# First chunk's q/k products tile by tile, with its statistics interleaved and the q/k weights in four column blocks

## The chip, the cores and the metric

The kernel runs on one core of one Trainium2 chip. The metric is the device time of one execution in microseconds (us), as a median over the executions of a kernel. The profile's span, from the first to the last instruction, is about 1.8 us shorter than that time. Ratios and intervals use fast executions alone.

## The reference

A sequence of 2048 rows of 512 numbers is normalised; a windowed attention runs beside a two-stage network with its own normalisation, and the two are multiplied. Cut to what matters here:

```python
x = A_x                                   # 1 x 2048 x 512, bf16
xn = _layernorm(x)                        # (x - mean) / sqrt(var + 1e-5)
qkv = (xn @ wqkv)                         # 512 x 1536: q, k, v; 32 heads of 16
logits = q . k over 8 keys, 2 apart, masked where the key lies before row 0
s = softmax(logits) @ v @ wo
h = gelu(_layernorm(xn) @ w1)             # a second layernorm of the same rows
...                                       # shifts, w2, third layernorm, w3, w4
return x + s * silu(...)
```

## The kernel before

Rows are worked on in four chunks (c = 0 to 3) of four tiles (j = 0 to 3) of 128 rows. The scheduling is manual: the order of the calls is the order of the instructions on each engine. For each tile, VectorE takes statistics, GpSimd raises to the power -0.5, VectorE normalises, TensorE transposes, ScalarE copies; then come the products with the q/k weights. The second layernorm needs no second pass: its factor follows from the first one's variance (`ln_again`), and is multiplied in by one large VectorE product for each chunk (`stage_m`), which the w1 products read.

```python
for c in range(NCH):                            # loads, all on the SP queue, in this order
    ...                                         # x of chunk c
    if c == 0:
        nc.sync.dma_start(out=wqk_sb[:, :, 0:D], in_=wqkv_v[:, :, 0:D])
        nc.sync.dma_start(out=wqk_sb[:, :, D : 2 * D], in_=wqkv_v[:, :, D : 2 * D])
    if c == 1:
        nc.sync.dma_start(out=w1_sb, ...)
...
def mask_coefs():                               # GpSimd, four small operations
def mask_poly(w):                               # GpSimd, three operations on 128x64
    gp.tensor_scalar(out=g, in0=c, scalar1=f2, scalar2=f1, op0=ALU.mult, op1=ALU.add)
    gp.tensor_tensor(out=g, in0=g, in1=c, op=ALU.mult)
    gp.tensor_scalar(out=g, in0=g, scalar1=f0, scalar2=None, op0=ALU.add)
def rsqrt_eps(dst, var):                        # chunks 1 to 3: L280 and L281
    nc.gpsimd.tensor_scalar(out=dst, in0=var, scalar1=EPS, scalar2=None, op0=ALU.add)
    nc.gpsimd.tensor_tensor(out=dst, in0=dst, in1=nhalf[...], op=ALU.pow)
def ln_first(j):                                # chunk 0, tile by tile
    nc.vector.bn_stats(...); nc.vector.bn_aggr(...)
    nc.vector.tensor_scalar(out=r, in0=mv[:, j, 1:2], scalar1=EPS, ...)
    nc.gpsimd.tensor_tensor(out=r, in0=r, in1=nhalf[:, 0:1], op=ALU.pow)
def stage_m(c):                                 # VectorE, the product of two SBUF inputs
    nc.vector.tensor_tensor(out=xn2T[c], in0=xnT[p][:, :, cs], in1=rrep..., op=ALU.mult)
...
    ln_first(0)
    ln_first(1)
    mask_coefs()
    first_n(0)                                  # norm 0
    first_t(0)                                  # transposes and copy
    warm(1)
    ...
    ln_first(2)
    mask_poly(0)
    parts = [qk_pair(0, a, 2) for a in range(3)]  # products in halves of 256 rows
    parts[0][0]()
    ...
    ln_again(0)
    mask_poly(1)
    ln_stats(1, 0, 2)
    ln_stats(1, 2, 4)
    ln_again(1)
    v_ones()                                    # two memsets on GpSimd
    ...
    stage_m(0)
    ln_norm(1)
    ...
    ln_stats(2, 0, 2); stage_w1(0, 0); ...; ln_stats(2, 2, 4); ln_norm(2)
    ...
    row_turn(2); turn(); row_fill(2)
    stage_m(1)
    ...
    stage_w1(1, 0)
```

The softmax here doesn't subtract the row's maximum and nothing guards it: scores larger than these inputs give would overflow.

## Time and profile before

| what | value |
|---|---|
| time, median of 3 | 203.36 us (203.36 to 203.42) |
| span of the profile | 201.7 us |
| TensorE busy | 194.3 us (96%) |
| VectorE, ScalarE, GpSimd busy | 133.8, 131.4, 73.3 us |
| TensorE dense from | 10.47 us on |
| w1 of chunk 1 starts | 27.51 us |

A line of the timeline reads: start, duration, engine, source line, operation, output and inputs with their shapes, how many instructions were joined, and in brackets the idle time just before with what ended it. A line of the chain reads: start, duration, what. PE is TensorE, DVE is VectorE, POOL is GpSimd.

### The profile page before, as it was taken

The numbers are of one execution on the slowest core, as the hardware profiler recorded it, in microseconds if no ns is written. First come the engines' busy times: TensorE is split into PE (matmuls) and PEld (weight loads), VectorE is DVE, ScalarE is ACT, GpSimd is POOL, SyncE is SP. The second block draws the span as 40 slices with busy tenths as digits, with TensorE's granted clock in tenths as the row PEclk, the third lists the DMA queues.
The fourth block names the chain that finished last, engine by engine and source line by source line (L and its number), as shares of the span: only waits on it lengthen the run. The fifth ranks groups of instructions, "written<-read, shape, count | busy, mean of one in ns | idle before, by whom it ended". The sixth has DMA issues, their size and how long they took to land.

```text
span 201.7 us, 4915 instructions
## 1 busy us (share of the span) xinstructions
PE 194.3 (96%) x1967; PEld 94.8 (47%) x1967; DVE 133.8 (66%) x263; ACT 131.4 (65%) x155; POOL 73.3 (36%) x146
## 2 busy tenths in 40 slices
PE   7699999999999999999999999999999999999991
PEld 2475445444444444444444444444445444444461
DVE  5788889734298988885560501288577968676683
ACT  2367665859988888896655566998788879222120
POOL 4789516300023095887364000001930590800000
PEclk9999999999999999999999999999999999999999
DMA  5993257367750086698657955789330141555221
GB/s 139 359 349 96 64 147 135 62 103 113 136 229 5 17 196 86 98 215 184 184 119 210 243 163 118 108 199 348 79 54 5 40 98 31 115 166 165 81 78 54
DMA packets 33734, 27.17 MB, mean 135 GB/s; under 512 B 14720, under 2 KB 31624, under 8 KB 33712
## 3 DMA queue, kind: packets, MB, share of 16 engines
q1 hardware_dynamic: 31520, 23.64, 46.0%
q0 software_dynamic: 2048, 3.09, 8.4%
q8 instruction: 15, 0.25, 0.6%
q10 hardware_dynamic: 144, 0.13, 0.2%
q14 instruction: 7, 0.06, 0.1%
HBM read 12.82 MB, written 4.98 MB: 88 GB/s over the span
## 4 chain that ended last, share of the span: by engine, by line
PE 91%; DVE 3%; POOL 2%; DMA 1%; issue 1%; ACT 0%; DVEq 0%
PE w_ps L567 19%; PE w_ps L530 17%; PE qk_ps L432 9%; PE v_ps L596 8%; PE w_ps L488 7%; PE w_ps L465 7%; PE s_ps L621 7%; PE wo_ps L742 7%; PE o_ps L644 5%; PE qk_ps L450 4%; PE w_ps L547 1%; DMA arena<-in_A_x_dram 1%; DVE l0s L311 1%; POOL l0r L315 1%; PE tr_ps L384 1%; DVE arena L747 1%
## 5 line engine op out<-in xcount | busy, mean ns | idle before, releaser
L626 ACT ACTIVATE arena<-s_ps 128x960 bf16<-128x960 f32 (+1 forms) x68 | 62.7, 975 | 12.3 <-PE s_ps L621 12.3
L567 PE MATMUL w_ps<-arena 128*128 128x512 bf16 (+1 forms) x173 | 40.1, 368 | 0.0
L534 ACT ACTIVATE arena<-w_ps 128x1024 bf16<-128x1024 f32 x20 | 20.5, 1025 | 13.3 <-PE w_ps L530 13.3
L686 POOL DMA_DIRECT2D arena<-orw x48 | 24.9, 526 | 5.3 <-DVE orw L656 5.3
L567 PEld LDWEIGHTS <-arena 128*128 128x128 bf16 x187 | 17.6, 98 | 18.9
L530 PEld LDWEIGHTS <-arena 128*128 128x128 bf16 x160 | 15.5, 98 | 19.2 <-issue 0.8
L752 POOL TENSOR_TENSOR arena<-arena 128x512 bf16<-128x512 bf16 x6 | 7.2, 1225 | 43.3 <-DVE arena L586 32.3
L432 PE MATMUL qk_ps<-arena 128*128 128x512 bf16 (+1 forms) x112 | 20.4, 333 | 0.5 <-ACT arena L328 0.5
L656 DVE CAST orw<-o_ps 128x960 bf16<-128x960 f32 (+1 forms) x17 | 19.7, 1157 | 1.5 <-PE o_ps L644 1.4
L601 DVE CAST v_aug<-v_ps 128x512 bf16<-128x512 f32 x17 | 11.7, 691 | 11.0 <-PE v_ps L596 11.0
L582 ACT ACTIVATE arena<-arena 128x512 bf16<-128x512 bf16 (+1 forms) x9 | 5.2, 583 | 20.4 <-DVE arena L573 20.4
L573 DVE TENSOR_TENSOR arena<-w_ps,arena 128x512 bf16<-128x512 f32 (+1 forms) x17 | 11.2, 659 | 10.3 <-PE w_ps L567 10.3
L530 PE MATMUL w_ps<-arena 128*128 128x512 bf16 x80 | 17.8, 379 | 0.1
L596 PE MATMUL v_ps<-wv_sb,arena 128*128 128x512 bf16 x68 | 17.5, 380 | 0.0
L530 PE MATMUL w_ps<-arena,arena 128*128 128x512 bf16 x80 | 17.4, 379 | 0.0
L621 PEld LDWEIGHTS <-arena 32*128 32x128 bf16 x544 | 10.2, 92 | 14.5 <-issue 14.4
L280 POOL TENSOR_SCALAR l3r<-l3m 128x1 f32<-128x1 f32 (+2 forms) x11 | 2.7, 244 | 38.6 <-DVE l3m L289 38.5
L621 PE MATMUL s_ps<-arena 32*128 32x120 bf16 (+1 forms) x544 | 15.9, 213 | 0.0
L488 PE MATMUL w_ps<-arena 128*128 128x512 bf16 x64 | 15.3, 380 | 0.0
L492 DVE TENSOR_TENSOR arena<-w_ps,arena 128x512 bf16<-128x512 f32 x16 | 10.4, 684 | 7.2 <-PE w_ps L488 7.2
L439 ACT CAST arena<-qk_ps 128x1024 bf16<-128x1024 f32 x11 | 11.1, 1019 | 6.0 <-PE qk_ps L432 6.0
L465 PE MATMUL w_ps<-arena 128*128 128x512 bf16 x64 | 14.8, 379 | 0.0
(108 smaller groups left out, 270.4 us busy)
## 6 DMA issues: line engine op xcount, KB each, us to landing
x1n_dram<-arena SPq DMA_DIRECT2D x5, 512.0 KB, 3.4
arena<-in_A_x_dram SPq DMA_DIRECT2D x4, 512.0 KB, 8.0
arena<-in_A_x_dram SPq DMA_DIRECT2D x6, 256.0 KB, 6.8
out_dram<-arena SPq DMA_DIRECT2D x6, 256.0 KB, 2.1
arena<-in_B_w_dram SPq DMA_DIRECT2D x1, 1376.0 KB, 6.7
arena<-in_B_w_dram SPq DMA_DIRECT2D x1, 1280.0 KB
arena<-arena SPq DMA_DIRECT2D x16, 72.0 KB, 2.5
arena<-arena SPq DMA_DIRECT2D x16, 68.0 KB, 3.0
```

Of the source, the lines that this page charges most:

```text
L432: nc.tensor.matmul(pt[:, b, hh * w : (hh + 1) * w], lhsT=wqk_sb[:, dt, nt * P : (nt + 1) * P], rhs=xnT[p][:, dt, k * CH + hh * w : k * CH ...
L465: nc.tensor.matmul(pt[:, b, :], lhsT=w1_sb[:, dt, g * P : (g + 1) * P], rhs=xn2T[c][:, dt, :], start=(dt == 0), stop=(dt == ND - 1),)
L488: nc.tensor.matmul(pt, lhsT=w2_src(p, g, m0), rhs=w2_sb[:, g, :], start=(g == 0), stop=(g == ND - 1))
L530: nc.tensor.matmul(pt[:, ft % 2, :], lhsT=w3_sb[:, dt, ft * P : (ft + 1) * P], rhs=x1nT[c][:, dt, :], start=(dt == 0), stop=(dt == ND - 1),)
L534: nc.scalar.activation(h3(c, 2 * a, 2), pt, AF.Gelu_apprx_tanh)
L567: nc.tensor.matmul(pt, lhsT=h3(c, ft, 1)[:, 0, jj * P : (jj + 1) * P], rhs=w, start=(ft == 0), stop=(ft == NF - 1),)
L596: nc.tensor.matmul(vp[:nk, :], lhsT=xnT[p][:, dt, k0 : k0 + nk], rhs=wv_sb[:, dt, :], start=(dt == 0), stop=(dt == ND - 1),)
L621: nc.tensor.matmul(st[:nk, b, i * nq : (i + 1) * nq], lhsT=kT[e][r : r + 32, dt, k0 : k0 + nk], rhs=qT[e][r : r + 32, dt, q0 : q0 + nq], s ...
L626: nc.scalar.activation(prv[:nk, 2 * h : 2 * h + 2], st[:nk, :, 0 : 4 * nq], AF.Exp, scale=SCALE)
L656: nc.vector.tensor_copy(out=orw[p, r][:, :, :, q0 - ra : q0 - ra + nq], in_=op[:, :, 0 : 4 * nq].rearrange("p j (s q) -> p j s q", q=nq),)
L686: nc.gpsimd.dma_start(out=oT[p][DH * hh : DH * (hh + 1), :, ra : ra + rw], in_=orw[p, r][32 * cg : 32 * cg + DH, jj],)
L742: nc.tensor.matmul(pt, lhsT=oT[p][:, dt, i * P : (i + 1) * P], rhs=wo_sb[:, dt, ds], start=(dt == 0), stop=(dt == ND - 1),)
```

## The change

The intent is to make TensorE dense earlier. Each tile's q/k products follow its transposes at once, as pieces of 128 columns; the statistics of the next tile are put between the steps of the tile before; the weights come in four column blocks so that the first products need not wait for a half. To clear the way for chunk 0's powers, the mask's coefficients and polynomials move behind chunk 1's statistics, and the two memsets go later still.

```diff
-            nc.sync.dma_start(out=wqk_sb[:, :, 0:D], in_=wqkv_v[:, :, 0:D])
-            nc.sync.dma_start(out=wqk_sb[:, :, D : 2 * D], in_=wqkv_v[:, :, D : 2 * D])
+            for n in range(0, 2 * D, 2 * P):
+                nc.sync.dma_start(out=wqk_sb[:, :, n : n + 2 * P], in_=wqkv_v[:, :, n : n + 2 * P])
 ...                       (first_s and first_a: ln_first in two parts;
 ...                        qk_first: a pair of products for columns lo to hi)
     ln_first(0)
-    ln_first(1)
-    mask_coefs()
+    first_s(1)
     first_n(0)
     first_t(0)
+    first_a(1)
+    first_s(2)
     warm(1)
     first_n(1)
     first_t(1)
-    warm(1)
-    ln_first(2)
-    mask_poly(0)
-    parts = [qk_pair(0, a, 2) for a in range(3)]
-    parts[0][0]()
-    ln_first(3)
+    first_a(2)
+    qa = [qk_first(a) for a in range(3)]
+    for a in range(3):
+        qa[a](0, P)
+    first_s(3)
     first_n(2)
     first_t(2)
-    parts[1][0]()
+    for a in range(3):
+        qa[a](P, 2 * P)
+    first_a(3)
 ...                       (tile 3 likewise)
     ln_again(0)
+    ln_stats(1, 0, 2)
+    mask_coefs()
+    qa[0](3 * P, CH)
+    stage_r(0)
+    for a in (1, 2):
+        qa[a](3 * P, CH)
+    ln_stats(1, 2, 4)
+    stage_m(0)
+    ln_again(1)
+    mask_poly(0)
     mask_poly(1)
-    ln_stats(1, 0, 2)
-    ln_stats(1, 2, 4)
-    ln_again(1)
-    v_ones()
 ...
     ln_again(2)
+    v_ones()
     stage_w1(0, 1)
```

More of the change, by code (lines that the diff above doesn't have):

```diff
@@ L309, in ln_first, with first_s, first_a @@
             lns[0] = [(0, TPC, first["mv"], first["r"])]
+        first_s(j)
+        first_a(j)
+    def first_s(j):
+        nc.vector.bn_stats(out=first["st"][:, j, :], in_=xn[0][:, j, :])
+    def first_a(j):
         st, mv, rstd = first["st"], first["mv"], first["r"]
-        nc.vector.bn_stats(out=st[:, j, :], in_=xn[0][:, j, :])
         nc.vector.bn_aggr(out=mv[:, j, :], in_=st[:, j, :])
@@ L443, in qk_pair, with qk_first, part @@
         return [lambda hh=hh: part(hh) for hh in range(halves)]
+    def qk_first(a):
+        pt = psa("qk_ps")
+        def part(lo, hi):
+            for b in range(2):
+                nt = 2 * a + b
+                for dt in range(ND):
+                    nc.tensor.matmul(
+                        pt[:, b, lo:hi], lhsT=wqk_sb[:, dt, nt * P : (nt + 1) * P],
+                        rhs=xnT[0][:, dt, lo:hi], start=(dt == 0), stop=(dt == ND - 1),
+                    )
+            if hi == CH:
+                dst, n0 = qk_dst(0, 2 * a)
+                nc.scalar.copy(out=dst[:, n0 : n0 + 2, 0:CH], in_=pt)
+        return part
     def qk_one(c, nt):
@@ L784 @@
     first_t(3)
-    parts[2][0]()
+    for a in range(3):
+        qa[a](2 * P, 3 * P)
     ln_again(0)
-    mask_poly(1)
-    ln_stats(1, 0, 2)
-    ln_stats(1, 2, 4)
-    ln_again(1)
-    v_ones()
-    parts[0][1]()
-    stage_r(0)
-    stage_m(0)
+    ln_stats(1, 0, 2)
[8 more added lines that the diff above has]
+    mask_poly(0)
+    mask_poly(1)
     ln_norm(1)
-    parts[1][1]()
-    parts[2][1]()
     qk_pair(0, 3)[0]()
```

## The prediction

> **What bounds the kernel now.** I read the page first (busy shares and the 40 slices), then the chain in order of time, then the timeline of the first 35 us by engine.
>
> ```profile
> PE 194.3 (96%) x1967; PEld 94.8 (47%) x1967; DVE 133.8 (66%) x263; ACT 131.4 (65%) x155; POOL 73.3 (36%) x146
> ...
> PE   7699999999999999999999999999999999999991
> ```
>
> TensorE is nearly never idle, except in the first two slices of 5.04 us, which is where the change works. The chain shows where the idle time stops:
>
> ```profile
> 9.42 0.55 POOL l0r L315
> 9.97 0.03 issue
> 10.00 0.42 DVE arena L319
> 10.42 0.04 issue
> 10.47 0.40 PE tr_ps L327 x4
> 10.87 1.75 PE qk_ps L432 x16
> 12.61 0.22 PE rrep_ps L406 x4
> 12.84 3.47 PE qk_ps L432 x24
> 16.31 1.73 PE w_ps L465 x8
> 18.04 0.89 PE tr_ps L384 x16
> 18.93 1.73 PE w_ps L465 x8
> 20.66 6.91 PE qk_ps L432 x32
> 27.56 3.56 PE w_ps L465 x16
> ```
>
> Until 10.47 us the end hangs on VectorE and GpSimd (statistics, power, norm of each of four tiles). From then on TensorE runs without a gap. So the most the change can give is how much earlier that dense stretch begins, as long as it then stays dense. The timeline shows a second limit almost hidden behind it:
>
> ```profile
> 22.20 0.73 POOL L281 TENSOR_TENSOR l1r<-l1r,nhalf 128x2 f32<-128x2 f32 x1
> 22.97 0.74 DVE L335 TENSOR_SCALAR arena<-arena,l1m,l1r 128x512 bf16<-128x512 bf16 x2 [0.28 <-POOL l1r L281]
> ...
> 25.95 0.31 DVE L345 STREAM_TRANSPOSE r2t<-r2w 128x128 bf16<-128x128 bf16 x1 [0.92 <-POOL r2w L374]
> 26.18 1.18 DVE L416 TENSOR_TENSOR arena<-arena 128x2048 bf16<-128x2048 bf16 x1
> ...
> 27.51 3.61 PE L465 MATMUL w_ps<-arena 128*128 128x512 bf16 x16
> ```
>
> The product L416 of chunk 1 ends at 26.18 + 1.18 = 27.36, and the w1 matmuls that read it start at 27.51. TensorE had only about 0.15 us to spare there. VectorE got there through chunk 2's norm, which waited for GpSimd's power at 22.97. If this side does not come earlier, TensorE cannot either.
>
> **What the Trainium skill says.** "TensorE: Matmul & The Clock Gate", section "Wait — 56ns, not 53.3ns?", gives warm start-to-start times of 55.6 ns at 128 columns and 215.7 ns at 512. The trace agrees: 16 transposes in 0.89 us are 55.6 ns each, 8 matmuls of 512 in 1.73 us are 216 ns each. "DMA: Bandwidth & Descriptors", section "Specifications", puts the smallest transfer for line rate at 512 B; the new weight blocks have rows of exactly 512 B instead of 1 KB, and no transfer of this trace has that size. "SBUF — State Buffer", section "SBUF: two separate sides", says that VectorE operations with two SBUF inputs and GpSimd operations exclude each other. The trace agrees:
>
> ```profile
> 14.31 1.18 POOL L280 TENSOR_SCALAR l1r<-l1m 128x2 f32<-128x2 f32 x1
> ...
> 34.57 2.30 POOL L374 TENSOR_TENSOR r2b<-r,nhalf 128x4 bf16<-128x4 f32 x1 [1.59 <-DVE r L368]
> ```
>
> The first takes 0.22 us elsewhere and the second 1.05; both began just after an L416 product (14.18 and 34.40) and lasted until it was done and their own time had passed.
>
> **The change part by part.**
>
> *The tiles' statistics.* After, VectorE does statistics 0, statistics 1, norm 0, aggregate 1, statistics 2, norm 1, and so on. Row durations: statistics 0.68, aggregate 0.18, small add 0.15, power on GpSimd 0.58, norm 0.41. From small add to power is 0.24, from power's end to norm 0.03, from a norm's start to the next VectorE start 0.32. Norm 0 no longer waits behind tile 1's aggregate: its power ends at 4.82, so it starts at 4.85 (5.07 before). Aggregate 1 follows at 5.17, add 5.38, power 5.62 to 6.20, norm 1 at 6.24 (5.94 before, so 0.3 later). Norm 2 then comes at 7.62 (8.28) and norm 3, behind the four small mask operations, at 9.03 (10.00). Tile 3 gains about 1.0 us.
>
> *The products.* The same 48 products of 256 columns become 96 of 128: at 55.6 against 108.5 ns (24 matmuls before: 16 x 0.1085 + 8 x 0.216 = 3.46) this adds 96 x 0.0556 - 48 x 0.1085 = 0.13 us of TensorE, and one warm-up matmul of 0.22 goes. In order: transposes 1 at norm 1 + 0.47 = 6.70; 24 products of tile 0 from 6.93 to 8.27; transposes 2 (ready 8.09) to 8.49; tile 1 to 9.83; transposes 3 (ready 9.58) to 10.05; tile 2 to 11.39; the first eight of tile 3 to 11.83; the row product to 12.06; 16 more to 12.95; the fourth pair 8 x 0.216 to 14.68. TensorE reaches w1 of chunk 0 at 14.7 instead of 16.31.
>
> *Whether w1 can start.* It needs the product L416, behind ScalarE's eviction (0.91 to the next start) and copy of the row (0.59): 11.87 + 0.91 + 0.59 + 0.05 = 13.4, ends 14.63. Just in time. So TensorE alone is 1.6 us ahead at this point.
>
> *The weights.* The loads drain in order. Summing the windows of 0.5 us gives 1.59 MB by 7.5 us, when both old halves are through; the second was landed about 0.65 later. The third new block (columns 512 to 767) completes the first 1.31 MB, read by some 6.65 and landed at 7.3, an estimate from these windows. It is needed at about 7.8. Rows of 512 B could eat that half microsecond, but no more than the slack that TensorE has later.
>
> *GpSimd.* This is where the change pays. Between the four powers GpSimd now idles, where it used to do the mask's coefficients (0.98) and first polynomial (1.41). These and the second polynomial (1.34) move behind chunk 1's statistics; the two memsets L273 (0.99) go later. Chunk 0's powers end at 8.97, its second rsqrt takes 2.02 to 10.99. Chunk 1's first pair waits for VectorE: 11.14 to 12.19; coefficients to 13.17; the second pair's L280 to 13.40. Its power (L281) would start at 13.49, as L416 starts at 13.4, and would be held until 14.63: end 15.36. Then chunk 1's second rsqrt, 2.55 as before, to 17.9; both polynomials to 20.65, or 21.2 as their last step meets the two-input mask add L241 at 20.07. Only then come chunk 2's statistics: first pair done 22.2, second 23.3.
>
> *Back on the path.* Before, that second pair was done at 22.93 and chunk 1's w1 began 27.51; now 23.3 makes w1 begin at 27.9. TensorE gets there at 20.66 - 1.6 + 6.91 = about 26.0 and waits nearly 2 us. Sum of this path: +0.4 us. If the power at 13.49 slips in just before L416, only 0.4 us instead of 1.2 is lost on GpSimd, the polynomials end near 20.0, chunk 2's second power near 22.6 and w1 begins at 27.2: -0.3 us. Everything after w1 follows TensorE and only shifts.
>
> **The rivals.**
>
> *The gain goes through.* VectorE, if GpSimd were never late, would reach chunk 1's L416 some 0.9 to 1.0 us earlier (its own work is unchanged; chunk 0's L416 comes 0.8 earlier and a wait of 0.28 goes). For it: the author moved the memsets out of GpSimd's way, and before, GpSimd only held norm 2 back by 0.28. Against it: 2.75 us of polynomials now sit exactly in front of the power that norm 2 waits for, and only 0.99 was taken out. It would give 202.4.
>
> *GpSimd takes the path* (worked out above). For it: GpSimd is busy 4.43 and 4.57 of 5 us in the windows 10 to 15 and 15 to 20. Against it: only small operations whose spans are rough. It gives 203.1 to 203.8.
>
> *The weights arrive late.* TensorE would wait for the third block near 7.8 us. Against it: even 0.5 us of lateness leaves TensorE 1 us ahead at w1 of chunk 1, where it waits anyway. Worth nothing, unless x of chunk 1 comes late too and delays the statistics, at most +0.3.
>
> *The clock.* Full speed was granted throughout; gaps before 7 us stay under 0.8 us. I give it nothing.
>
> **Range and chances.** The two forms of the GpSimd path give 203.36 + 0.4 and 203.36 - 0.3; the rival with the full gain gives 202.4. I weigh them 0.35, 0.4 and 0.25, mean 203.1 to 203.2, and take 203.2, range 202.4 to 203.9. 2% would be 4.1 us; the idle time that could be won at all is smaller, and no loss worked out comes near it: 0.01 faster, 0.98 same, 0.01 slower.
>
> **What would show it.** TensorE's dense stretch should begin at about 6.7 us instead of 10.5 and w1 of chunk 0 at 14.7 instead of 16.1; if it begins after 15.5, the steps for the tiles or the weights are wrong. A gap on TensorE of 1 to 2 us should stand ahead of chunk 1's w1, ended by VectorE's L416 product, and norm 2 should show a wait for GpSimd's power of chunk 2 of up to 1.5 us, with the polynomials ahead of that power. If there is no such gap and w1 of chunk 1 starts before 26.8, GpSimd's queue is not the bound and my main step is wrong; the time then falls to 202.4 or under. If weight loads of the first products wait for a transfer for more than 0.5 us, the 512 B rows cost more than I allowed. Chunk 0's products should take 55 to 57 ns each; 70 or more would refute the step for the narrower matmuls.

## More of the kernel before

The prediction shows the main lines. Three more matter later; they are from the timeline of the kernel before, and show where GpSimd does the mask's work, and when VectorE turns to chunk 1:

```profile
5.88 0.27 POOL L213 TENSOR_SCALAR co<-hot 128x3 f32<-128x3 f32 x1
...
8.01 0.40 POOL L224 TENSOR_SCALAR arena<-arena,co 128x64 bf16<-128x64 bf16 x1
...
11.98 0.40 POOL L224 TENSOR_SCALAR arena<-arena,hot,co 128x64 bf16<-128x64 bf16 x1
...
10.33 0.68 DVE L288 BATCH_NORM_STATS2 l1s<-arena 128x6 f32<-128x512 bf16 x1
```

The coefficients (from L213) and both polynomials (from L224) lie between and just behind chunk 0's powers, before chunk 1 has any statistics. VectorE begins chunk 1 without a wait: its rows were there.

## The result and the profile after

The changed kernel took 204.38 us (median of six executions; 204.3 without the slow one described next) against 203.38 us for the kernel before on the same chip. The ratio is 1.0045, with a 95% interval of 1.0029 to 1.0062. A ratio is the mean time of one kernel's fast runs over that of the other's of the same rounds, so it is not quite the ratio of the two medians. Five executions took 203.94 to 204.83 us. The sixth, the one that was profiled, took 1097.6 us. In it TensorE ran at about a sixth of its usual speed from beginning to end; this line of its timeline shows it:

```profile
192.31 24.06 PE L488 MATMUL w_ps<-arena 128*128 128x512 bf16 x18
```

That is 1.34 us for each matmul of 512 columns, against 0.216. VectorE's and GpSimd's busy times were as usual and the listed mean clock was 1.0. No other execution of any kernel here did this; its cause is open, and nothing below rests on it. So the first experiment ran the same kernel again, and its profile (203.63 us, span 201.9 us) is the profile after. Line numbers have shifted: L432 and L465 became L438 and L488, L335 became L341, L416 became L422, L374 became L380; L280, L281 and L288 kept theirs.

First TensorE, in the page's 40 slices of 5.05 us after:

```profile
PE   7799989999999999999999999999999999999992
```

The sixth slice shows an 8 where there was a 9: a new gap. The timeline after says what it is:

```profile
8.55 0.62 PE L458 MATMUL qk_ps<-arena 128*128 128x128 bf16 x8 [0.78 <-DMA arena<-in_A_wqkv_dram]
...
15.70 1.89 PE L488 MATMUL w_ps<-arena 128*128 128x512 bf16 x8
...
27.77 3.61 PE L488 MATMUL w_ps<-arena 128*128 128x512 bf16 x16 [0.66 <-DVE arena L422]
```

TensorE waits 0.78 us for the third weight block, reaches w1 of chunk 0 at 15.70 (16.14 in the same view before), and then waits 0.66 us for VectorE's product ahead of chunk 1's w1, which starts at 27.77 instead of 27.51.

Then VectorE, from the same timeline:

```profile
10.21 0.69 DVE L288 BATCH_NORM_STATS2 l1s<-arena 128x6 f32<-128x512 bf16 x1 [1.08 <-DMA arena<-in_A_x_dram]
...
22.20 0.73 DVE L341 TENSOR_SCALAR arena<-arena,l1m,l1r 128x512 bf16<-128x512 bf16 x2 [0.61 <-POOL l1r L281]
23.23 0.73 DVE L341 TENSOR_SCALAR arena<-arena,l1m,l1r 128x512 bf16<-128x512 bf16 x2 [0.29 <-POOL l1r L281]
...
26.44 1.18 DVE L422 TENSOR_TENSOR arena<-arena 128x2048 bf16<-128x2048 bf16 x1
```

VectorE has normed tile 3 at 8.71 (10.00 before), so it is 1.3 us ahead, but then waits 1.08 us for the rows of chunk 1. It keeps 0.1 us. Later chunk 2's norm waits for GpSimd twice, 0.61 and 0.29, where there was one wait of 0.28 before. GpSimd shows why:

```profile
12.00 0.23 POOL L280 TENSOR_SCALAR l1r<-l1m 128x2 f32<-128x2 f32 x1 [1.31 <-DVE l1m L289]
...
14.28 0.72 POOL L281 TENSOR_TENSOR l1r<-l1r,nhalf 128x2 f32<-128x2 f32 x1
...
18.07 0.39 POOL L224 TENSOR_SCALAR arena<-arena,co 128x64 bf16<-128x64 bf16 x1
...
20.28 0.45 POOL L226 TENSOR_SCALAR arena<-arena,hot 128x64 bf16<-128x64 bf16 x1
...
20.99 1.17 POOL L281 TENSOR_TENSOR l1r<-l1r,nhalf 128x2 f32<-128x2 f32 x1
```

GpSimd idles 1.31 us before 12.00, with work lying further back in its queue that it could have done then (coefficients 0.98 us, polynomials 2.66). It does the polynomials from 18.07 to 20.73 instead, and chunk 2's first power, which ended at 20.77 before, ends at 22.16. Finally the chain in order of time:

```profile
4.72 5.46 DMA arena<-in_A_x_dram
...
20.99 1.17 POOL l1r L281
...
26.44 1.19 DVE arena L422
27.77 3.61 PE w_ps L488 x16
```

Before, the chain was TensorE alone from 10.47 us on, past w1 of chunk 1. Now it runs from the transfer of chunk 1's rows over VectorE and GpSimd, and joins TensorE only at 27.77.

### The profile page after: what moved, and what is told of

It reads as the page before. It is cut to its first block, busy times and chain, and to the rows that moved or that the text cites. A ratio compares the mean times of both kernels' runs of the same rounds, so it can differ in the third digit from the quotient of the medians.

```text
span 1095.8 us, 4983 instructions
## 1 busy us (share of the span) xinstructions
PE 1064.7 (97%) x1986; PEld 315.6 (29%) x2014; DVE 134.8 (12%) x263; ACT 133.6 (12%) x155; POOL 72.1 (7%) x146
## 4 chain that ended last, share of the span: by engine, by line
PE 97%; issue 2%; DVE 0%; DVEq 0%
PE w_ps L590 20%; PE w_ps L553 19%; PE v_ps L619 8%; PE w_ps L511 8%; PE w_ps L488 8%; PE qk_ps L438 7%; PE wo_ps L765 7%; PE qk_ps L473 4%; PE s_ps L644 4%; PE o_ps L667 4%; PE qk_ps L458 3%; PE w_ps L570 1%; PE warm_ps L176 1%; PE tr_ps L390 1%; PE tr_ps L333 0%
## 5 line engine op out<-in xcount | busy, mean ns | idle before, releaser
L590 PE MATMUL w_ps<-arena 128*128 128x512 bf16 (+1 forms) x164 | 215.7, 1619 | 7.5 <-issue 7.5
L553 PE MATMUL w_ps<-arena 128*128 128x512 bf16 x78 | 104.4, 1697 | 1.9 <-issue 1.9
L553 PE MATMUL w_ps<-arena,arena 128*128 128x512 bf16 x78 | 104.3, 1711 | 1.9 <-issue 1.9
L590 PEld LDWEIGHTS <-arena 128*128 128x128 bf16 x187 | 55.8, 303 | 161.6 <-issue 161.6
L553 PEld LDWEIGHTS <-arena 128*128 128x128 bf16 x160 | 50.4, 317 | 159.1 <-issue 159.1
L619 PE MATMUL v_ps<-wv_sb,arena 128*128 128x512 bf16 x68 | 93.4, 1669 | 0.0
L438 PE MATMUL qk_ps<-arena 128*128 128x512 bf16 x61 | 83.9, 1707 | 2.8 <-issue 2.8
L488 PE MATMUL w_ps<-arena 128*128 128x512 bf16 x63 | 85.6, 1704 | 0.0
L511 PE MATMUL w_ps<-arena 128*128 128x512 bf16 x64 | 85.3, 1673 | 0.0
L473 PE MATMUL qk_ps<-arena 128*128 128x512 bf16 x32 | 46.6, 1626 | 8.4 <-issue 8.4
L644 PE MATMUL s_ps<-arena 32*128 32x120 bf16 (+1 forms) x544 | 45.5, 588 | 0.0
L765 PE MATMUL wo_ps<-arena,arena 128*128 128x512 bf16 x30 | 42.0, 1678 | 2.8 <-issue 2.8
L765 PE MATMUL wo_ps<-arena 128*128 128x512 bf16 (+1 forms) x35 | 44.3, 1560 | 0.0
L667 PE MATMUL o_ps<-arena,v_aug 128*32 128x120 bf16 (+1 forms) x544 | 43.6, 616 | 0.0
L438 PEld LDWEIGHTS <-arena 128*128 128x128 bf16 x64 | 21.1, 331 | 59.4 <-issue 58.4
L488 PEld LDWEIGHTS <-arena 128*128 128x128 bf16 x64 | 20.4, 320 | 60.3 <-issue 60.1
L765 PEld LDWEIGHTS <-arena 128*128 128x128 bf16 x68 | 20.9, 310 | 58.3 <-issue 58.3
```

What stands on the lines that cost most here:

```text
L438: nc.tensor.matmul(pt[:, b, hh * w : (hh + 1) * w], lhsT=wqk_sb[:, dt, nt * P : (nt + 1) * P], rhs=xnT[p][:, dt, k * CH + hh * w : k * CH ...
L473: nc.tensor.matmul(pt, lhsT=wqk_sb[:, dt, nt * P : (nt + 1) * P], rhs=xnT[p][:, dt, cs], start=(dt == 0), stop=(dt == ND - 1),)
L488: nc.tensor.matmul(pt[:, b, :], lhsT=w1_sb[:, dt, g * P : (g + 1) * P], rhs=xn2T[c][:, dt, :], start=(dt == 0), stop=(dt == ND - 1),)
L511: nc.tensor.matmul(pt, lhsT=w2_src(p, g, m0), rhs=w2_sb[:, g, :], start=(g == 0), stop=(g == ND - 1))
L553: nc.tensor.matmul(pt[:, ft % 2, :], lhsT=w3_sb[:, dt, ft * P : (ft + 1) * P], rhs=x1nT[c][:, dt, :], start=(dt == 0), stop=(dt == ND - 1),)
L590: nc.tensor.matmul(pt, lhsT=h3(c, ft, 1)[:, 0, jj * P : (jj + 1) * P], rhs=w, start=(ft == 0), stop=(ft == NF - 1),)
```

## The experiments

Three theories were tested. The first: the order of GpSimd's queue moves the end, because it puts the polynomials in front of the power that chunk 2's norm needs. The second: the four weight blocks arrive late and hold TensorE, and the rows of chunk 1 behind them. The third, added later: the new gap on TensorE costs more than its length, because the clock is lowered after it. The kernel before had medians of 203.39, 203.46 and 203.45 us in the three groups of runs (e1 to e4, e5 to e8, e9 to e12).

One reading goes through all of them. Where TensorE is dense behind w1 of chunk 1, span minus that start must be a constant:

| kernel | w1 of chunk 1 starts | span | difference |
|---|---|---|---|
| before | 27.51 | 201.7 | 174.2 |
| e1 (the change) | 27.77 | 201.9 | 174.1 |
| e2 | 27.84 | 202.0 | 174.2 |
| e3 | 27.25 | 201.4 | 174.2 |
| e5 | 26.79 | 200.9 | 174.1 |
| e10 | 28.27 | 202.4 | 174.1 |
| e12 | 26.48 | 200.6 | 174.1 |

So it is this one start that sets the end in these kernels; e4, e6 and e8 fit as well (174.1 to 174.2). Three others, e7, e9 and e11, show a larger difference, and each has its reason below.

### e1: the change again

No edit.

> The changed kernel once more, for a profile in the fast state (the first one fell into an execution with TensorE at about a sixth of its speed). Three theories for the 0.9 us by which it is slower. G: GpSimd's queue. The two polynomials stand before the power of chunk 2 that norm 2 waits for; TensorE reaches w1 of chunk 1 early and waits 1 to 2.5 us for the product on VectorE. W: the weights in four blocks. The first load of x of chunk 1 lands about 1.3 us later (the statistics of chunk 1 waited 1.01 us for it and began at 10.35 in the slow profile, which the TensorE clock does not touch), so everything behind these statistics is later. C: the clock. The fast runs of the changed kernel list a granted clock of 0.997 to 1.000 against 1.000 before; 0.003 of 202 us at half speed is up to 0.6 us. Time 204.0 to 204.6 under all three; a gap on TensorE ahead of w1 of chunk 1 under G and W, none but a low clock under C.

Measured: 203.77 us (203.63 to 206.1), ratio 1.0043 (1.0011 to 1.0076). The loss is real and small, and its size varies: four of the six executions lie within 203.63 to 203.79, the others are 204.65 and 206.1. The profiled one gave the readings above: +0.26 us at w1 and +0.2 us of span.

### e2: the change with the weights in two halves

```diff
-            for n in range(0, 2 * D, 2 * P):
-                nc.sync.dma_start(out=wqk_sb[:, :, n : n + 2 * P], in_=wqkv_v[:, :, n : n + 2 * P])
+            nc.sync.dma_start(out=wqk_sb[:, :, 0:D], in_=wqkv_v[:, :, 0:D])
+            nc.sync.dma_start(out=wqk_sb[:, :, D : 2 * D], in_=wqkv_v[:, :, D : 2 * D])
```

> The change without its split of the weights: two loads of 512 columns, as before. W: x of chunk 1 lands by 9.0 us again, its statistics begin at about 9.4, GpSimd is 0.9 us earlier all along, and the time falls to about 203.3. G: the polynomials still stand in front; GpSimd gets a little earlier where it had waited for the statistics, so 203.5 to 204.0. C: no change, 204.0 to 204.6.

Measured: 203.49 us (203.13 to 203.91), ratio 1.0004 (0.9992 to 1.0015). In the profiled execution, its slowest, TensorE waited even longer for the weights:

```profile
9.34 0.62 PE L458 MATMUL qk_ps<-arena 128*128 128x128 bf16 x8 [1.27 <-DMA arena<-in_A_wqkv_dram]
```

TensorE was dense from there on, and reached w1 of chunk 1 at 27.84 without a wait. So the weights alone can hold it as far back as GpSimd does. Undoing the blocks saves about 0.3 us in the medians and brings the kernel back to the time of the kernel before, but to no gain: TensorE, held by the weights, and VectorE, held by GpSimd (its product ends at 27.69), reach w1 of chunk 1 at nearly the same time.

### e3: GpSimd's order mended, four blocks kept

The coefficients and the first polynomial go into the gaps between chunk 0's powers, and the second polynomial goes behind chunk 0's second root, ahead of chunk 1's statistics. Nothing else changes.

```diff
     ln_first(0)
+    mask_coefs()
     first_s(1)
 ...
     first_a(1)
+    mask_poly(0, (0, 1))       # its first two operations
     first_s(2)
 ...
     first_a(2)
+    mask_poly(0, (2,))         # its third
 ...
     ln_again(0)
+    mask_poly(1)
     ln_stats(1, 0, 2)
-    mask_coefs()
 ...
     ln_again(1)
-    mask_poly(0)
-    mask_poly(1)
```

> The change with the mask's coefficients and polynomials put into GpSimd's gaps between the four powers (each about 0.8 us) and behind chunk 0's second rsqrt, where GpSimd waited 1.24 us; the weights stay in four blocks. G: chunk 2's power is done some 2 to 3 us earlier, norm 2 no longer waits for it, w1 of chunk 1 begins near 26.5 and the time falls to 202.3 to 202.9. W: x is still late, the time stays at 203.7 or more. C: no change, 204.0 to 204.6.

Measured: 202.63 us (202.5 to 203.13), ratio 0.9965 (0.9952 to 0.9978). That is faster than the change and than the kernel before. GpSimd and VectorE in its timeline:

```profile
21.29 0.56 POOL L283 TENSOR_SCALAR l1r<-l1m 128x2 f32<-128x2 f32 x1 [1.53 <-DVE l1m L292]
...
25.92 1.18 DVE L425 TENSOR_TENSOR arena<-arena 128x2048 bf16<-128x2048 bf16 x1
```

GpSimd is no longer late: it waits 1.53 us for VectorE before chunk 2's second pair (L283 and L425 here are L280 and L422 of the change). The product starts at 25.92 instead of 26.44 and w1 at 27.25. Moving only GpSimd's order brought 1.1 us of median time against the change, so the first theory holds. TensorE still waited 0.61 us for the third block, until 8.75, and is dense after that: it now ends the path.

### e4: GpSimd's order mended, weights in two halves

The edits of e2 and e3 together.

> Both edits together. G alone: as the run with the gaps alone, 202.3 to 202.9, since the statistics of chunk 1 have slack once GpSimd is free. W alone: as the run with two blocks, about 203.3. Both at work: the lowest of the four, 202.0 to 202.6. C: no change.

Measured: 203.4 us (203.25 to 203.91), ratio 1.0007 (0.9995 to 1.0019). With GpSimd out of the way, the halves cost 0.8 us against e3 in the medians. In the profiled execution TensorE waited for the second half until 8.87 and ran densely from there to w1 at 27.36. The profiled execution of e3, its slowest (203.13 us), is only 0.2 us shorter, with the third block at 8.75; its usual 202.6 us presumably had the block earlier, which no profile shows. By the medians the blocks do what they were meant to do; the change could not show it, as GpSimd held the path.

### e5: GpSimd mended, third pair postponed

The third block is needed only by the third pair of products. So the first two pairs of tile 1 go before it.

```diff
-    for a in range(3):
+    for a in range(2):
         qa[a](0, P)
 ...
     first_t(2)
-    for a in range(3):
+    for a in range(2):
         qa[a](P, 2 * P)
+    qa[2](0, 2 * P)
```

> The gaps kernel with the third pair of products (its weights land last) moved behind tile 1's first two pairs, so that TensorE has other work until 9.2 us. In the gaps kernel TensorE waited 0.61 us for the third weight block, until 8.75, and from there ran densely to w1 of chunk 1 at 27.27 with VectorE's product ready only 0.17 us before. Weights theory: this wait goes, TensorE is some 0.4 to 0.6 us earlier at w1 of chunk 0 and the time falls to 202.0 to 202.4. Rival: VectorE's own chain behind the late x of chunk 1 now binds at w1 of chunk 1, and the time stays within 0.2 us of the gaps kernel's 202.63.

Measured: 202.63 us (202.54 to 202.7), ratio 0.9961 (0.9949 to 0.9973). TensorE no longer waits for weights; it is dense from 8.31 us, and w1 of chunk 1 starts at 26.79. The median equals e3's, but the executions agree better (0.16 us apart, against 0.63): the postponement seems to take away e3's slower executions, of which the profiled one was one (its span is 0.5 us longer). With five executions of each this is not shown. In the profile GpSimd's power was held in this run too (1.89 us at 14.07 instead of 0.72), and nothing came of it: with no polynomials behind it, GpSimd still had 1.32 us to wait before chunk 2's second pair.

### e6: the same with the weights in two halves

The edits of e2, e3 and e5 together.

> The same with the weights in two loads of 512 columns. Its third pair is needed at 9.2 us and the second half landed at 8.83 and 9.30 in the two profiles with two loads. Weights theory: hardly any wait is left, so it equals or beats the same kernel with four blocks, 201.9 to 202.4, where without the postponement it was 0.8 us behind. If two loads are bad for another reason it stays at 203.2 or more.

Measured: 202.66 us (202.56 to 203.21), ratio 0.9967 (0.9955 to 0.9979). Postponing makes the halves good enough: the loss of e4 is gone. What counts is that nothing waits for the third quarter of the weights, not how many blocks bring it.

### e7: the change with only the postponement

The diff of e5, without that of e3.

> The changed kernel itself with only that postponement: polynomials still ahead of chunk 2's power. GpSimd theory: TensorE's 0.78 us wait for weights was not what set the end, since it waited again for VectorE ahead of w1 of chunk 1; no gain, 203.5 to 204.3. Weights theory as the whole cause: 203.0 to 203.3.

Measured: 204.18 us (203.64 to 206.51), ratio 1.0036 (1.0022 to 1.005). TensorE lost its wait for the weights and the time did not fall. In the one execution with a profile, the reason is that GpSimd got later still. The timeline and then the windows of the profiled execution (206.51 us, the slowest), whose columns are stretch, length, busy time of PE, PEld, DVE, ACT and POOL with counts, granted clock, DMA share and GB/s:

```profile
13.92 1.39 POOL L214 TENSOR_SCALAR co<-co 128x1 f32<-128x1 f32 x1
...
28.96 5.30 PE L488 MATMUL w_ps<-arena 128*128 128x512 bf16 x16 [2.16 <-DVE arena L422]
```

```profile
31.00:33.00 2.00, 2.00 (x6) 0.76 (x5) 1.93 (x5) 1.03 (x1) 1.19 (x3) 0.50 0.99 226
```

The rows of chunk 1 came only at 10.73, and the product of chunk 0, at 13.94, met a coefficient operation on GpSimd that takes 0.31 us elsewhere. It began 0.02 us ahead by the record and still took 1.39. w1 of chunk 1 started at 28.96. After the 2.2 us of idle TensorE the granted clock was 0.72 in the half microsecond from 30.0, 0.50 from 30.5 to 33.5 and 0.86 in the half after; 16 matmuls took 5.30 us instead of 3.61. This is the 1.6 us or so by which e7's difference of span and start (175.7) is larger. The third theory has one execution for it, then, and e10 and e11 ask whether it is the rule.

### e8: the kernel before with the weights in four blocks

```diff
-            nc.sync.dma_start(out=wqk_sb[:, :, 0:D], in_=wqkv_v[:, :, 0:D])
-            nc.sync.dma_start(out=wqk_sb[:, :, D : 2 * D], in_=wqkv_v[:, :, D : 2 * D])
+            for n in range(0, 2 * D, 2 * P):
+                nc.sync.dma_start(out=wqk_sb[:, :, n : n + 2 * P], in_=wqkv_v[:, :, n : n + 2 * P])
```

> The kernel before with only the weights in four blocks. Its statistics of chunk 1 begin at 10.33 anyway, after the late landing of 10.2 to 10.35, and its third pair reads the third block at 10.7 only. So nothing waits: 203.2 to 203.6. If the split costs by itself (x or weights too late also here), 203.8 or more.

Measured: 203.32 us (203.29 to 203.34), ratio 0.9995 (0.9983 to 1.0007). The blocks by themselves change nothing in the kernel before, since nothing there waits for them. They do slow the transfers. Two lines of the windows from 5 to 10 us, the first of the kernel before, the second of the change:

```profile
5.00:10.00 5.00, 3.52 (x30) 2.26 (x30) 3.82 (x15) 1.76 (x3) 3.87 (x10) 1.00 1.07 359
```

```profile
5.00:10.00 5.00, 3.89 (x53) 3.15 (x52) 3.81 (x16) 1.74 (x3) 2.65 (x7) 1.00 0.98 295
```

The last column is GB/s. All nine kernels with four blocks (rows of 512 B) moved 279 to 318 GB/s in this window, e8 304; all four with halves (rows of 1 KB) moved 338 to 359. The rows of chunk 1 stand behind the weights in the same queue. By the traces' semaphore records, the first of them landed at 8.98 in the kernel before and at 10.39 in e8, where only the blocks differ. Landing scatters, though: 9.80 to 10.71 in the nine with four blocks and 8.97 to 10.04 in the four with halves, and the 10.04 is e2's, so that its shorter wait for them (0.70 us instead of 1.08) shows little. A rival was not tested: four issues keep the SP queue longer than two, so that the rows' load was issued at 4.72 instead of 3.62. By then only some 0.7 MB of the 1.57 MB ahead of it had been moved in e1 (summed from half-microsecond windows), which speaks against it.

### e9: chunk 1's product ahead of chunk 2's row

The product needs nothing of chunk 2's row, which waits for GpSimd (`r2w`, 0.91 us of VectorE idle). So it goes first. The load of chunk 2's transposed rows (`turn`) goes ahead of the row as well, which is a second change.

```diff
-    row_turn(2)
+    stage_m(1)
     turn()
+    row_turn(2)
     row_fill(2)
-    stage_m(1)
```

> The changed kernel with chunk 1's product (VectorE) moved ahead of the turn of chunk 2's row, which waits 0.9 us for GpSimd, and chunk 2's load through the transposing queue moved ahead of that row too. Polynomials and weights stay as in the change. If the path GpSimd's power of chunk 2, norm 2, second rsqrt, row turn, product of chunk 1, w1 of chunk 1 is what sets the end, the product starts about 1.2 us earlier, TensorE's gap ahead of w1 of chunk 1 nearly goes and the time falls to 202.9 to 203.3. If something else holds it: 203.6 to 204.3.

Measured: 203.93 us (202.99 to 205.43), ratio 1.0047 (1.0012 to 1.0081). The expected time was missed, the expected start was met. TensorE's timeline:

```profile
26.75 3.61 PE L488 MATMUL w_ps<-arena 128*128 128x512 bf16 x16 [0.19 <-DVE arena L422]
...
31.65 1.89 PE L438 MATMUL qk_ps<-arena 128*128 128x512 bf16 x8 [0.42 <-DMA arena<-x1n_dram]
```

w1 of chunk 1 starts at 26.75, a whole microsecond earlier than in e1, which confirms what stood in front of it. Then the gain is given back: chunk 2's transposed rows hold TensorE 0.42 us at 31.65, and chunk 2's row, now behind the transposing load on SP, was filled only by a load issued at 31.73; w1 of chunk 2 waits 0.33 us more for its product at 36.49.

The edit lies after 19 us, so the start of this execution is one more sample of the change itself, one in which the weights came in time:

```profile
13.93 1.76 POOL L281 TENSOR_TENSOR l1r<-l1r,nhalf 128x2 f32<-128x2 f32 x1
```

With no wait for weights, VectorE's product began at 13.77 instead of 14.31, just ahead of GpSimd's power, which took 1.76 us instead of 0.72. Chunk 2's norm came at 22.38 and 23.41, later than e1's 22.20 and 23.23. By e1's distance of 3.21 us from the second norm to the product, the old order would have put w1 at about 27.95 (an estimate). By this estimate, from one execution of each, TensorE ahead by half a microsecond makes the end of the change no earlier, and rather later.

### e10: the memsets back in front of the polynomials

This adds 0.98 us to GpSimd's queue on the disputed path.

```diff
     ln_again(1)
+    v_ones()
     mask_poly(0)
 ...
     ln_again(2)
-    v_ones()
```

> The suspected cost made larger: the changed kernel with the two memsets (0.99 us on GpSimd) put back ahead of the polynomials. GpSimd path: exactly 0.99 us more, 204.7 to 205.3 where the clock stays. Clock: the gap on TensorE ahead of w1 of chunk 1 grows from 1.1 to 2.2 us to 2.1 to 3.2 us, so in half or more of the executions TensorE falls to half speed for one stretch behind it, and these take 206.3 to 207. If GpSimd is not on the path: 203.6 to 204.3.

Measured: 204.45 us (204.13 to 205.09), ratio 1.0054 (1.0042 to 1.0067). The median stayed below the time expected. In the profiled execution, the fastest, w1 of chunk 1 starts at 28.27, 0.50 later than in e1 and not 0.98: GpSimd was 0.29 ahead of e1 at its second root, as the rows came earlier (9.83), lost 0.31 on a polynomial step that VectorE held, and did not lose the 0.45 that e1's power at 20.99 was held for. The direction is as the first theory says. TensorE was idle 1.45 us ahead of w1 and the clock stayed at full. The six executions lie within 0.96 us, so none shows an excess of 1.6 us like e7's. So the third theory is refuted as a general cause.

### e11: e10 with the gap filled

Eight matmuls of 512 columns on constants ahead of chunk 1's w1 keep TensorE busy in the gap.

```diff
     ln_norm(3, slice(0, 1))
+    fp = pst("b", "fill_ps")
+    for _ in range(8):
+        nc.tensor.matmul(fp[:, 0, :], lhsT=ones_bf[:], rhs=..., start=True, stop=True)
     stage_w1(1, 0)
```

> The same with eight matmuls of 512 columns on constants (8 x 0.216 = 1.73 us, their result is not used) ahead of w1 of chunk 1, in TensorE's gap. Clock theory: TensorE is no longer idle for over 1.5 us, no execution falls to half speed, all lie at 204.7 to 205.3. If the slow executions come from something else, such as late transfers, they stay as frequent as in the run without the fill.

Measured: 206.29 us (205.9 to 209.1, that last one slow; 205.95 without it), ratio 1.0136 (1.0122 to 1.0151). The expectation was missed. In the profiled execution the weights came in time, GpSimd's power collided with the product (1.73 us at 13.99), a polynomial step was held as well (0.90 instead of 0.39), w1 started at 28.95, and 0.89 us of wait for chunk 2's transposed rows followed at 34.32. Whether the fill helps the clock, this run does not tell.

### e12: the best of it

Four blocks; the coefficients divided over two gaps so that no power of chunk 0 is delayed; the third pair postponed (e5); chunk 1's product first (e9).

```diff
     ln_first(0)
+    mask_coefs(0)              # two operations
 ...
     first_a(1)
+    mask_coefs(1)              # the other two
+    mask_poly(0, (0,))
 ...
     first_a(2)
+    mask_poly(0, (1, 2))
 ...                            (and the edits of e5 and e9)
```

> A candidate for the best: coefficients and polynomials in GpSimd's gaps, the coefficients divided so that they no longer hold up tile 1's power by 0.19 us; third pair postponed; product of chunk 1 first. TensorE is dense from tile 2's transposes, which come 0.2 us earlier than in the kernel with gaps and postponement: 202.3 to 202.6 against 202.63. If VectorE binds instead, 202.6.

Measured: 202.41 us (202.09 to 202.86), ratio 0.9953 (0.9941 to 0.9965). This beats both kernels: the kernel before by 1.0 us in the medians. Its timeline:

```profile
24.23 1.22 DVE L427 TENSOR_TENSOR arena<-arena 128x2048 bf16<-128x2048 bf16 x1
...
26.48 2.32 PE L493 MATMUL w_ps<-arena 128*128 128x512 bf16 x10
```

The product (L427 here) is over at 25.45, a microsecond before TensorE comes for it, and TensorE is dense from 8.11 us on. Here the gain that the change was made for goes through.

## Why the prediction was right or wrong

The time on record was 203.2 us within 202.4 to 203.9. The median of the first job (the result above), 204.3 to 204.4, lies outside the range, and that of the second (e1), 203.77, inside it at the upper edge. The sign was wrong: the change makes the kernel slower by about 0.4% (ratios 1.0045 and 1.0043). "Within 2%" was right.

**The tiles' statistics: right.** Norms were to come at 4.85, 6.24, 7.62 and 9.03; they came at 4.64, 6.01, 7.36 and 8.71, with the intervals as worked out within 0.06 us and the first tile landed 0.2 us earlier.

**The products: right in size.** 24 products took 1.34 us from one start to the next group's, about 56 ns each; 70 or more, the sign of failure named, was far off.

**The weights, and with them the slip-in form's -0.3: the step that failed.** The prediction had the third block landed at 7.3 and called its lateness "Worth nothing, unless x of chunk 1 comes late too and delays the statistics, at most +0.3." Both happened: the block let TensorE go on only at 8.55, and the rows of chunk 1 let VectorE begin at 10.21 instead of some 9.4. Summed from the half-microsecond windows of e1, the 1.31 MB were through at about 6.9 us instead of 6.65, and landing took a further 1.6 instead of 0.65. So the lower rate is the smaller part, and the landing, taken over from loads in halves, the larger. The prediction saw that the rows of 512 B "could eat that half microsecond" and did not carry it on to the rows behind the weights. The lateness moved GpSimd's first pair of chunk 1 from 11.14 to 12.00, and TensorE's w1 of chunk 0 from 14.7 to 15.70; the gain of 1.6 us on TensorE was 0.4. In e1 GpSimd's power slipped in ahead of the product, for which the prediction had w1 of chunk 1 at 27.2; it came at 27.77. So the form that was to bring -0.3 us brought +0.26 at w1. Two things lie in these 0.6 us and are not separated: the polynomials ended 0.73 us later (20.73 against "near 20.0"), and the power behind them was then held 0.45 us by VectorE's two-input mask add (L241, from 20.93), a collision that the prediction counted in its other form only. Two of the prediction's own signs of failure were met: w1 of chunk 0 after 15.5, and a wait for weights of more than 0.5 us (0.78).

**GpSimd takes the path: right as a mechanism.** The gap ahead of chunk 1's w1, ended by VectorE's product, is there (0.66 us and not "1 to 2", as TensorE was later too). Chunk 2's norm waits for the power, with the polynomials ahead of it. The worse form's 27.9 was met by 27.77, and e3, which mends only this, gained 1.1 us.

**The two forms and their weights: wrong.** The prediction gave 0.4 to the power slipping in ahead of the product, for -0.3 us. In e1 it did slip in, at 14.28 against the product's 14.31, and the time still rose, as everything had started 0.9 us later. In e9 and e11 it did not slip in and took 1.76 and 1.73 us. In these profiles of the change, which one happened went with the wait for the weights: after 0.78 us of it (e1) and 0.27 (e10, 13.90 against 14.03) the power was first, after none the product. There the two delays shut each other out, and neither branch led to a gain. It is no general rule: in e7, whose TensorE waits for no weights, late rows and a held operation came together. The branch of -0.3 and the rival of 202.4 "with the full gain" together held 0.65 of the weight, and none of the change's eleven fast executions came near either (the lowest took 203.63); without them the prediction's own +0.4 would have read 203.8, close to e1.

**The clock: given nothing, mostly right.** The lowered clock explains some 1.6 us of e7's profiled 206.51 us. e1's 206.1 us has no profile; its listed mean clock was 1.0, where e7's was 0.991, which speaks against the same cause. It is not the rule (e10).

What stays open: the first job's five fast executions lie 0.2 to 1.1 us above e1's usual 203.7 and have no profile of their own. The collisions of e9 and e11 would be of the size to explain some of that, but for those executions it is only argued. The 1097.6 us execution is unexplained.

## What to carry to other kernels

Work that is moved out of one critical stretch has to land in an idle one: before moving small operations on a helper engine, list that engine's idle gaps and what it releases next, because here some 2.7 us of harmless polynomials in front of one power cost more than the reordering gained. When a change splits a load, look also at what is queued behind that load. A transfer that is late can hide a collision (e9), and removing a wait need not make a kernel faster (e7); mend the engine that ends the path first, then the earlier waits.

## What the Trainium skill lacked or had wrong

- "DMA: Bandwidth & Descriptors", section "Specifications", puts the smallest transfer for line rate at 512 B. Here the same window of 5 to 10 us, in which other loads run too, moved less with weight rows of exactly 512 B than with rows of 1 KB: 279 to 318 GB/s in nine kernels against 338 to 359 in four. No page has how much the landing of one load differs between executions of the same program: the third quarter of the weights held TensorE for 0.78, 0.27 and 0 us in three executions with the same program up to there (e1, e10, e9).
- "TensorE: Matmul & The Clock Gate", section "HAM oscillation", gives idle gaps of more than about 3.4 us as what lowers the clock. Here some 2.2 us of idle were followed by 3 us at a granted clock of 0.50 (e7), while 1.45 us were not (e10). One profile of each is too little for a threshold.
- The same page, section "Seeing it yourself", tells of a clock stuck at a quarter for over 50 us. Here a whole execution of 1097.6 us ran at 1.34 us for each 512-column matmul, a sixth of the usual speed, with a listed mean clock of 1.0; no page has this.
